# Spectral filter and gated MLP on one core: side work dealt out over more gaps, a block's low parts in one VectorE operation

## The chip, the core and the metric

One core of a Trainium2 chip runs the whole program. The metric is device time in microseconds (us) from a run of the compiled kernel, the median over several runs. Beside them stands one profiled execution, whose trace gives every duration below.

## The reference

The input `A_x` has 2048 tokens of 576 features. Two branches are mixed by a gate for each token:

```
g = sigmoid((x * gate_w).sum(-1, keepdims=True))
a = irfft2(rfft2(x) * (w_r + 1j * w_i), s=(2048, 576))
b = (gelu(x @ w_gate) * (x @ w_up)) @ w_down        # 576 -> 4608 -> 576, gelu by tanh
out = g * a + (1 - g) * b
```

## The kernel before, in words

**TensorE and its precision.** Every matmul of the MLP is done on operands split into a high part, rounded to the format of the fast matmul, and a low part, the rest. Three matmuls (high by high, low by high, high by low) stand for one. So every operand, weights, tokens and hidden values alike, must first be split: ScalarE copies the high part (`copy`, line 238), VectorE subtracts it from the source for the low part.

**Passes, tiles, blocks.** The tokens are worked in two passes of 1024 (p = 0, 1). The 36 tiles of 128 hidden features go in 18 pairs i. The first pairs of a pass (3 in the first, 7 in the second, `FIRST`) are *normal*: for each half tb of the tokens, `hidden` runs 14 matmuls for the gate and 14 for the up product of a tile, then GELU, product and split follow on ScalarE and VectorE. All later pairs are *blocks* (`products`): a Strassen-like scheme takes seven products of 2x2 block combinations in place of eight, named a11, a12, s2, s3, a22, s1, s4, in this order (n = 0 to 6, two halves s of seven matmuls each, `seven`, line 1178). The weights' combinations are made by `Block.prep` (line 1153): `total` adds quadrants on VectorE (line 1165), `high` copies 768 columns on ScalarE, `rest_of` makes the low parts on VectorE, 512 columns at line 1172 and a half-height piece of 256 columns at line 1173. There are three slots for such weights, and product m+2 is prepared while m runs. The tokens' combinations are made once for a pass by `operands` and `other_operands`, and the last one, s4, by `last_operand` just before the first block.

**Down projections.** `down` multiplies one 128-token part of the hidden values by two `dn` tiles: 12 matmuls of 288 columns into a `pdn` bank, ScalarE scales the result by 1-g into a `stg` tile (line 938), and GpSimd's queue adds it to the tile's sum `yd` in DRAM (line 920).

**The spectral branch** is side work, with no matmuls but for the column transform: `gate_part` and `other_gates` make the gates of the two halves, `forward_rows` the row transforms (VectorE), `send_away` puts rows into DRAM as `away`, `columns` takes them back as `til`, does the column transform with matmuls at line 300 and the filter, `inverse_rows` goes back and adds a to `yd`.

**The order is written out by hand** (a manual schedule): each engine runs its instructions in the order in which the program issues them. `gap()` (line 707) is called after every seven matmuls or so and counts time in gaps. `at(n, fn)` puts a step n gaps later, `seq` a chain of such steps, `due` runs what is left of a chain before its result is needed. The generator of the side work (`gens`) is advanced in a gap while `credit` is positive: TensorE's time times `RATE` 1.08 is put in, VectorE's costs are taken out, and what is saved up is capped at 3.0 us. `waits(n)` lets the generator pass n gaps. A second list, `side`, is served when the generator only waits. An instruction whose operand is late holds what is written behind it for its engine. SyncE's queue (SP) issues nearly all loads and stores in the same manner, and a `dma_start` whose buffer is not free yet holds the loads behind it.

**Kept low parts.** `lows` are DRAM tiles in which the first pass stores low parts of weights (`lower`, line 792): those of all 36 `dn` tiles, and of the first six `gub` tiles. The second pass loads them back on GpSimd's queue (line 796) instead of computing them.

## Time and profile before

| | |
|---|---|
| runs | 1398.64 us median of 3 (1397.9 to 1405.32) |
| profiled execution | 1401.8 us, its span 1400.0 us |
| busy share of the span | TensorE 96%, VectorE 83%, ScalarE 57%, GpSimd 21% |
| instructions | 20396, of them 7322 matmuls and 7322 weight loads |
| DMA | 272.12 MB, mean 194 GB/s; GpSimd's queue 44.7% and SP's 34.6% of the DMA engines' time |

How to read it: PE is TensorE, PEld its weight load, DVE VectorE, ACT ScalarE, POOL GpSimd, SP SyncE. In a group's row stand the line, the engine, the operation, the tiles written and read, shapes and count, then busy us and mean ns of one, then the engine's idle time just before them and what ended most of it. In a timeline row stand the start, the duration, engine, line, operation and count, and in brackets the idle time before it with what ended it. PEclk is the granted share of TensorE's clock. The spans of matmuls overlap, so TensorE counts as busy also where its clock is halved.

### The profile page before, as it was taken

The numbers are of one execution on the slowest core, as the hardware profiler recorded it, in microseconds if no ns is written. First come the engines' busy times: TensorE is split into PE (matmuls) and PEld (weight loads), VectorE is DVE, ScalarE is ACT, GpSimd is POOL, SyncE is SP. The second block draws the span as 40 slices with busy tenths as digits, with TensorE's granted clock in tenths as the row PEclk, the third lists the DMA queues.
The fourth block names the chain that finished last, engine by engine and source line by source line (L and its number), as shares of the span: only waits on it lengthen the run. The fifth ranks groups of instructions, "written<-read, shape, count | busy, mean of one in ns | idle before, by whom it ended". The sixth has DMA issues, their size and how long they took to land.

```text
span 1400.0 us, 20396 instructions
## 1 busy us (share of the span) xinstructions
PE 1349.6 (96%) x7322; PEld 1177.7 (84%) x7322; DVE 1166.2 (83%) x1772; ACT 797.4 (57%) x1302; POOL 287.3 (21%) x370
## 2 busy tenths in 40 slices
PE   9998999989999999999999999999899998999998
PEld 7887888878888888878888878888688887888887
DVE  6998999779999988766388767879889966999994
ACT  5557556545565566676556555743565575556552
POOL 0021111112111111111302222221122241222231
PEclk9999999999999999999999999999999999999999
DMA  9785667867777678988989999868667788667798
GB/s 338 246 170 101 137 143 175 237 194 147 147 147 147 147 181 225 282 219 225 309 276 279 234 235 238 208 140 248 196 144 141 144 166 215 118 145 147 147 211 227
DMA packets 119237, 272.12 MB, mean 194 GB/s; under 512 B 14560, under 2 KB 24800, under 8 KB 116832
## 3 DMA queue, kind: packets, MB, share of 16 engines
q0 software_dynamic: 48864, 106.06, 44.7%
q1 hardware_dynamic: 70272, 164.76, 34.6%
q8 instruction: 57, 0.93, 0.3%
q14 instruction: 44, 0.36, 0.1%
HBM read 144.43 MB, written 119.19 MB: 188 GB/s over the span
## 4 chain that ended last, share of the span: by engine, by line
PE 60%; DVE 16%; issue 11%; DMA 7%; ACT 4%; POOL 2%; SPq 0%; DVEq 0%; ACTq 0%; POOLq 0%
PE pdn L907 20%; PE pgu L1186 14%; PE px L1186 11%; PE pgu L1188 2%; DMA tmp<-xg 2%; PE px L1188 2%; PE pgu L828 2%; PE pgu L829 2%; PE pgu L830 2%; DVE gub L1172 2%; DMA ext<-til 1%; PE px L828 1%; PE px L829 1%; PE px L830 1%; DMA til<-ext 1%
## 5 line engine op out<-in xcount | busy, mean ns | idle before, releaser
L920 POOL DMA_DIRECT2D yd<-stg x264 | 226.4, 879 | 1045.6 <-ACT stg L938 1013.4
L938 ACT ACTIVATE stg<-pdn,omg 128x576 f32<-128x576 f32 x276 | 200.8, 737 | 213.5 <-PE pdn L907 196.1
L907 PEld LDWEIGHTS pdn<-dn,hb 128*128 128x128 f32 x2184 | 304.5, 188 | 11.4 <-DVE low L969 0.4
L907 PE MATMUL pdn<-dn,hb 128*128 128x288 f32 x2184 | 312.8, 294 | 0.1
L1186 PE MATMUL pgu<-xhi,gub 128*128 128x512 f32 x624 | 202.3, 405 | 26.2 <-ACT gub L238 11.1
L238 ACT ACTIVATE gub<-low 128x768 fp32r<-128x768 f32 (+3 forms) x180 | 155.7, 865 | 22.5 <-DVE low L1165 11.7
L1186 PE MATMUL px<-til,gub 128*128 128x512 f32 x624 | 160.7, 393 | 3.3 <-ACT xraw L238 3.3
L1186 PEld LDWEIGHTS pgu<-xhi,gub 128*128 128x128 f32 x624 | 114.5, 192 | 54.0 <-ACT gub L238 12.9
L1186 PEld LDWEIGHTS px<-til,gub 128*128 128x128 f32 x624 | 114.1, 188 | 27.5 <-ACT xraw L238 6.3
L1186 PE MATMUL pgu<-xlo,gub 128*128 128x512 f32 x312 | 124.6, 399 | 0.0
L1172 DVE TENSOR_TENSOR gub<-low,gub 128x512 fp32r<-128x512 f32 x156 | 107.3, 688 | 10.4 <-ACT gub L238 8.9
L907 PE MATMUL pdn<-dn,ext 128*128 128x288 f32 x624 | 100.8, 295 | 1.8 <-DVE ext L892 1.8
L907 PE MATMUL pdn<-dn,gub 128*128 128x288 f32 x624 | 99.9, 296 | 1.7 <-ACT stg L938 1.7
L907 PEld LDWEIGHTS pdn<-dn,gub 128*128 128x128 f32 x624 | 93.0, 189 | 7.7 <-ACT stg L938 1.9
L828 PE MATMUL pgu<-xhi,gub 128*128 128x512 f32 x240 | 93.9, 391 | 0.0
L829 PE MATMUL pgu<-xhi,gub 128*128 128x512 f32 x240 | 93.9, 391 | 0.0
L830 PE MATMUL pgu<-xlo,gub 128*128 128x512 f32 x240 | 93.6, 390 | 0.0
L907 PEld LDWEIGHTS pdn<-dn,ext 128*128 128x128 f32 x624 | 88.7, 188 | 2.9 <-DVE ext L892 2.9
L1186 PE MATMUL pgu<-til,gub 128*128 128x512 f32 x312 | 79.9, 391 | 0.0
L1218 DVE TENSOR_TENSOR xraw<-xraw,pgu 128x512 f32<-128x512 f32 x104 | 69.6, 682 | 8.4 <-PE pgu L1188 8.4
L1165 DVE TENSOR_TENSOR low<-low 128x768 f32<-128x768 f32 x75 | 71.5, 955 | 1.3
L1186 PEld LDWEIGHTS pgu<-xlo,gub 128*128 128x128 f32 x312 | 60.3, 193 | 13.8
(211 smaller groups left out, 2464.7 us busy)
## 6 DMA issues: line engine op xcount, KB each, us to landing
yd<-stg POOLq DMA_DIRECT2D x264, 288.0 KB, 5.3
low<-ws SPq DMA_DIRECT2D x87, 384.0 KB, 5.7
gub<-wd SPq DMA_DIRECT2D x52, 288.0 KB, 4.0
low<-wgu SPq DMA_DIRECT2D x17, 640.0 KB, 7.2
lo<-dn SPq DMA_DIRECT2D x36, 288.0 KB, 5.4
dn<-lo POOLq DMA_DIRECT2D x36, 288.0 KB, 6.6
rows<-col POOLq DMA_DIRECT2D x32, 256.0 KB, 7.2
gub<-ws SPq DMA_DIRECT2D x17, 384.0 KB, 6.2
```

Of the source, the lines that this page charges most:

```text
L238: act.activation(o, i, AF.Copy)
L828: pe.matmul(ps, w[:, 0, k, c], xhi[tb][:, k], start=k == 0, stop=False)
L829: pe.matmul(ps, w[:, 1, k, c], xhi[tb][:, k], start=False, stop=False)
L830: pe.matmul(ps, w[:, 0, k, c], xlo[tb][:, k], start=False, stop=False)
L907: pe.matmul(ps[half], h[:, l, c], d[:, q, half * HD:(half + 1) * HD], start=part == 0 and n == 0, stop=part == 1 and n == 2)
L920: pl.dma_start(yd[u], o, accum_op=ALU.add)
L938: put(u, lambda o: act.activation(o.rearrange("p (c k) -> p c k", c=2), v[:, :, 0:HD], AF.Copy, scale=omg[:, u:u + 1]), i == 0)
L1165: vec.tensor_tensor(o, p, q, ALU.subtract)
L1172: vec.tensor_tensor(w[:, 768:1280], x[:, 0:512], f(w[:, 0:512]), ALU.subtract)
L1186: pe.matmul(ps, l[:, c], x[:, t], start=first and t == 0 and q == 0, stop=False, skip_group_check=True)
L1188: pe.matmul(ps, w[:, 512 + P * s:512 + P * (s + 1)], xt, start=False, stop=True, skip_group_check=True)
L1218: vec.tensor_tensor(o, o, v, ALU.add)
```

## The change

- `Block.prep`: the low parts are laid out so that one VectorE operation of 3x256 columns writes all of them. For this the high part is copied by two ScalarE operations, 2x256 columns and 256 columns scaled by a column of the mask `msk` (0 for the upper half of the partitions, 1 for the lower).
- First block of a pass: products 0, 1 and 2 are prepared during the last normal pair (leads 0, 2 and 4) in place of 0 in that pair, 1 at its end and 2 within the block. `last_operand` takes seven gaps in place of three.
- `finish` in the blocks: product and split of the hidden values are put one or two gaps later, except for c22 and the last pair. The high copies of a block's `dn` tiles move from n = 2, 3 to n = 4, 5.
- Gates of the second half are made from the `rows` tile that was loaded for the row transform, with strided reads. The separate loads `xg` are gone. The gates of the first half run beside `operands` as side work, and the first operand loads `xs` are issued earlier, ahead of the weight loads of tiles 2 and 3.
- `split`, `tails_of` and `other_operands` issue one step of each kind in a gap, and the stores of `other_operands` and `send_away` are issued two gaps after the work that makes them. The cap on saved-up credit is 2.0 in place of 3.0.
- `away` is one DRAM tile. `til` comes back in four loads by digit, put 1, 6, 18 and 26 gaps after product 5 of the last block of the first pass; before, it came in four contiguous loads after that block. The column transform may start 14 gaps after that point. Weight loads for tiles NT+2 and NT+3 come later.
- `inverse_rows` of the second half waits 13 and 9 gaps for its two loads, in place of 6 and 6.
- `lows` keeps only `dn` tiles 14 to 35. In the second pass the low parts of `gub` tiles 0 to 5 and `dn` tiles 0 to 13 are computed.

The matmuls and their order are the same.

```diff
-        away = [dram.tile([P, 4 * SW], F32, name=f"away{i}", tag=f"away{i}") for i in range(6)]
+        away = dram.tile([P, 16 * SW], F32, name="away", tag="away")
+        spilt = [dram.tile([P, 4 * SW], F32, name=f"spilt{i}", tag=f"spilt{i}") for i in range(2)]
...
-                nc.sync.dma_start(away[2 * h + e], tmp[:, 0:4 * SW])
-                yield from waits(5)
+                at(2, lambda e=e: nc.sync.dma_start(away[:, 4 * SW * (2 * h + e):4 * SW * (2 * h + e + 1)],
+                                                    tmp[:, 0:4 * SW]))
+                yield from waits(7)
...
                 for e in range(2):
-                    nc.sync.dma_start(tmp[:, 0:4 * SW], away[4 + e])
-                    yield from waits(6)
+                    nc.sync.dma_start(tmp[:, 0:4 * SW], spilt[e])
+                    yield from waits(9 if e else 13)
...
-            gw = tmp[:, 0:D]
-            xg = [tmp[:, D * (1 + i):D * (2 + i)] for i in range(3)]
+            gw = tmp[:, D:2 * D]
             nc.sync.dma_start(gw, a["gw"][0:1, :].to_broadcast([P, D]))
-            for t in range(3):
-                nc.sync.dma_start(xg[t], a["xg"][t])
-            yield from waits(5)
+            yield from waits(9)
+            one, fin = gate_part(1, gw)
             for t in range(8):
-                gate_sum(8 + t, xg[t % 3], xg[t % 3], gw)
-                yield 0.78
-                if t + 3 < 8:
-                    at(1, lambda t=t: nc.sync.dma_start(xg[t % 3], a["xg"][t + 3]))
-                yield None
-            gate_part(1)[1]()
+                one(t)
+                yield 1.33
+            fin()
...
-            side.append(forward_rows())
-            yield from operands()
-            yield from side.pop()
             yield from send_away(0)
...
-            credit[0] = min(credit[0], 3.0)
+            credit[0] = min(credit[0], cap[0])
...
-        lows = [[dram.tile([P, n], F32, name=f"lo{j}_{n}", tag=f"lo{j}_{n}") if n == D or j < KEPT else None
-                 for n in (KT * 256, D)] for j in range(NT)]
+        lows = {j: dram.tile([P, D], F32, name=f"lo{j}", tag=f"lo{j}") for j in range(2 * FIRST[1], NT)}
...
         def split(xs, his, los):
-            for x, h in zip(xs, his):
-                copy(h, x)
-            yield None
-            yield None
-            for x, h, l in zip(xs, his, los):
-                vec.tensor_tensor(l, x, f(h), ALU.subtract)
-                yield 0.72
+            for k in range(len(xs) + 2):
+                if k < len(xs):
+                    copy(his[k], xs[k])
+                if k > 1:
+                    vec.tensor_tensor(los[k - 2], xs[k - 2], f(his[k - 2]), ALU.subtract)
+                    yield 0.72
+                yield None
...
             for i in range(3):
-                yield from sums(1, i, cells[0:5], [fr(c) for c in cells[8:11]])
-                xs, his = [cells[q] for q in (3, 0, 2)], [fr(c) for c in cells[5:8]]
-                nc.sync.dma_start(four_d[:, TB * i:TB * (i + 1)], cells[4])
+                q, h = quads[i], [fr(c) for c in his[i]]
...
                 if i == 2:
+                    out += [(kept[3 + n], cells[8 + n]) for n in range(3)]
+                    yield from tails_of(list(zip(h, xs)))
+                    out += [(kept[n][:, 2048:], f(h[n])) for n in range(3)]
+                else:
+                    yield from split(xs, h, [fr(x) for x in xs])
                     for n in range(3):
-                        nc.sync.dma_start(kept[3 + n], cells[8 + n])
-                    yield from tails_of(list(zip(his, xs)))
-                    for n in range(3):
-                        nc.sync.dma_start(kept[n][:, 2048:], f(his[n]))
-                else:
-                    los = [fr(x) for x in xs]
-                    yield from split(xs, his, los)
-                    for n in range(3):
-                        nc.sync.dma_start(kept[n][:, TB * i:TB * (i + 1)], f(his[n]))
-                        nc.sync.dma_start(kept[n][:, 1024 + TB * i:1024 + TB * (i + 1)], f(los[n]))
-                    yield from waits(3)
+                        out += [(kept[n][:, TB * i:TB * (i + 1)], f(h[n])),
+                                (kept[n][:, 1024 + TB * i:1024 + TB * (i + 1)], xs[n])]
+                at(2, lambda out=out: store(out))
+                if i == 0:
+                    at(6, lambda: load_xs(1, 2, quads[2]))
+            yield from waits(3)
...
-            def high():
-                for i in range(2):
-                    copy(hi[:, i], fourth[i])
-                next(todo), next(todo)
-
-            def rest_of():
-                for i in range(2):
-                    vec.tensor_tensor(lo[:, i], fourth[i], f(hi[:, i]), ALU.subtract)
-                    credit[0] -= 0.72
-                for _ in todo:
-                    pass
-
-            at(1, high)
-            at(3, rest_of)
+            def high(i):
+                copy(hi[:, i], fourth[i])
+
+            def low(i):
+                vec.tensor_tensor(lo[:, i], fourth[i], f(hi[:, i]), ALU.subtract)
+                credit[0] -= 0.72
+
+            def tail(n):
+                for _ in range(n):
+                    next(todo, None)
+
+            at(1, lambda: tail(2))
+            at(2, lambda: high(0))
+            at(3, lambda: high(1))
+            at(4, lambda: tail(2))
+            at(6, lambda: [tail(2), low(0)])
+            at(7, lambda: low(1))
...
                 def high():
-                    copy(w[:, 0:768], x)
+                    copy(w[:, 1:4:2], x[:, 0:3:2])
+                    act.activation(w[:, 2], x[:, 1], AF.Copy, scale=msk[:, 1:2])
 
                 def rest_of():
-                    vec.tensor_tensor(w[:, 768:1280], x[:, 0:512], f(w[:, 0:512]), ALU.subtract)
-                    vec.tensor_tensor(w[64:128, 512:768], x[64:128, 512:768], f(w[64:128, 512:768]), ALU.subtract)
-                    credit[0] -= 1.15
+                    vec.tensor_tensor(w[:, 0:5:2], x, f(w[:, 1:4]), ALU.subtract)
+                    credit[0] -= 1.0
 
...
-                    seq((name, p, i), (1, gelu), (2, mult), *split_h(o, hold, wants))
+                    soon = 0 if name == "c22" or end else 1
+                    high, low = (fn for _, fn in split_h(o, hold, wants))
+                    seq((name, p, i), (1, gelu), (2 + soon, mult), (4 + soon - end, high), (5 + 2 * soon, low))
...
-                b.prep(i + m // 7, m % 7)
+                if n or i > b.first:
+                    b.prep(i + m // 7, m % 7)
+                if n == 0 and i > b.first:
+                    b.load_d(i)
+                if p and n in (1, 2):
+                    lower(("dn", j + n - 1), dn[(j + n - 1) % 4], None, 0)
+                if n in (4, 5):
+                    w, x = dn[(j + n - 4) % 4], b.wdr[n - 4]
+                    copy(w[:, 0], x)
+                    if p == 0:
+                        lower(("dn", j + n - 4), w, x, 0.76)
+                if n == 3 and i == b.first:
+                    b.more()
                 if n == 0:
                     b.load(i + 1, "r11", "r21")
-                if n in (2, 3):
-                    w, x = dn[(j + n - 2) % 4], b.wdr[n - 2]
-                    copy(w[:, 0], x)
-                    lower(("dn", j + n - 2), w, x, 0.76)
-                if n == 3 and i == b.first:
-                    b.more()
-                if n == 4:
-                    due(("dn", j))
-                    due(("dn", j + 1))
-                    b.load_d(i + 1)
...
+            if n == 5:
+                til = mk("til", [16 * SW])
+                there, here = (x.rearrange("p (e d k) -> p d e k", d=4, e=4) for x in (away, til))
+                for d, n in enumerate((1, 6, 18, 26)):
+                    at(n, lambda d=d: nc.sync.dma_start(here[:, d], there[:, d]))
+                back[0] = count[0] + 14
             if n == 6:
                 load_w(NT + 1)
-                load_w(NT + 2)
...
-        for j in range(2):
-            at(11 + j, lambda j=j: nc.sync.dma_start(lows[j][0], f(gub[j][:, KT * 256:])))
-        aux += [lambda: None] * 2
+        aux += [lambda: None, lambda: load_xs(0, 0, [xraw[:, q] for q in range(4)])]
...
         for i in range(2):
             aux.append(lambda i=i: [prep_dn(i), due(("dn", i)), load_w(i + 2)])
-        aux += [lambda: None] * 4
-
-        def branch():
-            one, fin = gate_part(0)
+        def gates():
+            one, fin = gate_part(0, gwb)
             for t in range(8):
                 one(t)
                 yield 1.33
             fin()
             for u in range(4):
-                at(max(1, 26 + u - count[0]), lambda u=u: release(u))
+                at(max(1, 22 + u - count[0]), lambda u=u: release(u))
+            yield from forward_rows()
+
+        def branch():
+            at(4, lambda: side.append(gates()))
+            yield from operands()
+            yield from side.pop()
             yield from spectral()
 
         aux.append(lambda: gens.append(branch()))
...
             if last and tb == 1:
                 b.wide()
-                b.prep(b.first, 0)
+                for m in range(2):
+                    b.prep(b.first, m, 2 * m)
...
+            if last and tb == 1:
+                b.prep(b.first, 2, 4)
             h1, key1 = hidden(j + 1, tb, mid)
...
                 b.load_d(b.first)
-                b.prep(b.first, 1)
                 last_operand()
...
-                til = mk("til", [16 * SW])
-                for e in range(4):
-                    at(3 + 2 * e, lambda e=e: nc.sync.dma_start(til[:, 4 * SW * e:4 * SW * (e + 1)], away[e]))
                 for n in range(6):
                     down(*pend.pop(0))
                     if n == 2:
+                        load_w(NT + 2)
                         prep_dn(NT)
                         prep_gu(NT + 1)
                         prep_dn(NT + 1)
-                        load_w(NT + 3)
-                back[0] = count[0] + 12
+                        at(6, lambda: load_w(NT + 3))
```

On the ScalarE queue at the opening of the first pass's blocks (the names `gub_70` and `gub_71` are the weight slots of the block products, `xhi_64` and `xtl_68` the parts of s4, `px` a copy of a product that frees its bank), before:

```order
L238 ACTIVATE hb_81<-gl_83 128x512
L238 ACTIVATE xhi_64<-ext 128x512 x2
L238 ACTIVATE xtl_68<-xraw 128x512
L238 ACTIVATE px_1146<-pgu 128x512
L238 ACTIVATE gub_70<-low 128x768
L238 ACTIVATE gub_71<-low 128x768
L238 ACTIVATE px_1147<-pgu 128x512
```

and with the change:

```order
L931 ACTIVATE stg_86<-pdn,omg 128x576
L238 ACTIVATE gub_70<-low 128x2x256
L1188 ACTIVATE gub_70<-low,msk 128x256
L113 ACTIVATE tmp<-rows 128x320 x2
L238 ACTIVATE gub_71<-low 128x2x256
L1188 ACTIVATE gub_71<-low,msk 128x256
L931 ACTIVATE stg_87<-pdn,omg 128x576
L113 ACTIVATE tmp<-rows 128x320 x2
L124 ACTIVATE rows<-tmp 128x20x8
L125 ACTIVATE rows<-tmp 128x20x8
L931 ACTIVATE stg_88<-pdn,omg 128x576
L238 ACTIVATE hb_81<-gl_83 128x512
```

The copies of the weights for products 1 and 2 moved from behind the copies for s4 to ahead of two evacuations of down projections (`stg_87`, `stg_88`) that precede the block.

On VectorE, at the same place, before (line 1172 and line 1173 make the low parts of a block product, line 93 is a butterfly of the row transform, line 1165 a combination of quadrants):

```order
L93 TENSOR_TENSOR tmp<-rows 128x1280
L1165 TENSOR_TENSOR low<-low 128x768 x2
L93 TENSOR_TENSOR rows<-rows 128x40x32
L1172 TENSOR_TENSOR gub_70<-low,gub_70 128x512
L1173 TENSOR_TENSOR gub_70<-low,gub_70 64x256
L1165 TENSOR_TENSOR low<-low 128x768
```

and with the change, where the low parts of product 1 are the row of line 1191:

```order
L127 SCALAR_TENSOR_TENSOR rows<-rows,tmp 128x20x8
L885 TENSOR_TENSOR hb_80<-gl_82,hb_80 128x512
L1191 TENSOR_TENSOR gub_70<-low,gub_70 128x3x256
L129 SCALAR_TENSOR_TENSOR rows<-rows,tmp 128x20x8
L863 TENSOR_TENSOR gl_83<-gl_83,pgu 128x512
```

The low parts of product 1 moved from behind two butterflies to ahead of the last up product's multiplication (`gl_83`).

On SP's queue around the load of the second half's rows (`xn`), before:

```order
L571 DMA away_98<-tmp 128x2320
L653 DMA rows<-xn 128x4608
L660 DMA tmp<-gw 128x576
L662 DMA tmp<-xg 128x576 x3
L803 DMA lo_576_146<-dn_75 128x576
L1148 DMA gub_1143<-wd 128x576 x2
L1143 DMA low<-ws 128x768
L668 DMA tmp<-xg 128x576
```

and with the change:

```order
L571 DMA away<-tmp 128x2320
L654 DMA rows<-xn 128x4608
L660 DMA tmp<-gw 128x576
L1155 DMA low<-ws 128x768
L1155 DMA gub_1111<-ws 128x768
```

The eight loads `xg` are gone, and the block's quadrants (`ws`) follow the rows directly.

83 lines of the change are left out of this document (53 added, 30 removed).

## The prediction

> **What bounds the kernel now.** I read the page's head first, then who waited for whom on TensorE, then the granted clock, then the timeline at each long wait.
>
> ```profile
> span 1400.0 us, 20396 instructions
> PE 1349.6 (96%) x7322; PEld 1177.7 (84%) x7322; DVE 1166.2 (83%) x1772; ACT 797.4 (57%) x1302; POOL 287.3 (21%) x370
> ```
>
> TensorE is the bound, and the change leaves its 7322 matmuls as they are. So a gain can only come out of time in which TensorE stands still or runs at half clock. The waits of TensorE alone, longest in total first:
>
> ```profile
> PE pgu L1186 <- ACT gub L238: 11.1, 7, 3.1
> PE px L300 <- ACT til L238: 7.4, 10, 1.6
> PE px L1186 <- ACT xraw L238: 5.9, 7, 2.1
> PE pgu L1186 <- DVE gub L1172: 5.6, 2, 4.1
> PE pgu L1186 <- ACT px L238: 5.1, 1, 5.1
> PE pgu L1186 <- ACT ext L238: 2.9, 4, 1.0
> PE pdn L907 <- DVE ext L892: 1.8, 3, 0.9
> ```
>
> These seven rows make 39.8 us; the rows below them are 1.7 us and less each, some 5.6 us in all. The windows view, asked for the four stretches at half clock, gives the rest (columns: the stretch, its length, busy time of PE, PEld, DVE, ACT and POOL, granted clock, DMA share, GB/s):
>
> ```profile
> 123.33:130.16 6.83, 5.82 (x14) 4.57 (x15) 6.71 (x11) 2.27 (x4) 0.00 (x0) 0.50 0.07 12
> 297.41:300.82 3.41, 3.41 (x10) 2.65 (x9) 3.37 (x7) 0.28 (x1) 0.29 (x1) 0.50 0.94 287
> 986.90:993.73 6.83, 5.49 (x13) 4.33 (x14) 6.70 (x11) 1.62 (x3) 0.00 (x0) 0.50 0.63 238
> 1171.22:1178.05 6.83, 5.07 (x15) 4.39 (x16) 6.45 (x12) 3.84 (x7) 1.73 (x2) 0.50 0.57 169
> ```
>
> TensorE was busy 19.8 us in them at clock 0.50, so half of that, 9.9 us, is lost to the clock. Waits and clock together are 45.4 + 9.9 = 55.3 us, 4% of the span: this is what there is to win. Each half-clock stretch follows one long wait, and the timeline shows what was late there. Opening of the blocks, first pass:
>
> ```profile
> 119.34 1.14 ACT L238 ACTIVATE xhi<-ext 128x512 fp32r<-128x512 f32 x2
> 120.38 0.62 ACT L238 ACTIVATE xtl<-xraw 128x512 fp32r<-128x512 f32 x1
> 121.42 1.74 ACT L238 ACTIVATE gub<-low 128x768 fp32r<-128x768 f32 x2
> 122.30 0.51 PE L1186 MATMUL pgu<-xhi,gub 128*128 128x512 f32 x1 [3.13 <-ACT gub L238]
> 124.34 0.80 PE L1186 MATMUL pgu<-xhi,gub 128*128 128x512 f32 x1 [1.54 <-DVE gub L1172]
> ```
>
> The weights of product 1 are copied after three copies for s4, which is needed only at n = 6. TensorE waits 3.13 us for the copy and 1.54 us for the low part. Second pass, same place:
>
> ```profile
> 983.65 0.50 PE L1186 MATMUL pgu<-xhi,gub 128*128 128x512 f32 x1 [1.37 <-ACT gub L238]
> 988.24 0.79 PE L1186 MATMUL pgu<-xhi,gub 128*128 128x512 f32 x1 [4.09 <-DVE gub L1172]
> ```
>
> The third is the return of the second half's rows, the fourth the gates of the second half:
>
> ```profile
> 1163.78 0.33 SPq L621 DMA_DIRECT2D tmp<-away  x1
> 1170.68 1.77 ACT L238 ACTIVATE rows<-tmp 128x289 f32<-128x289 f32 x3 [5.99 <-DMA tmp<-away]
> 1172.98 1.22 PE L1186 MATMUL pgu<-xhi,gub 128*128 128x512 f32 x2 [5.08 <-ACT px L238]
> ```
>
> ```profile
> 291.98 0.76 DVE L736 SCALAR_TENSOR_TENSOR tmp<-tmp 128x576 f32<-128x576 f32 x1 [4.89 <-DMA tmp<-xg]
> 294.56 0.63 ACT L238 ACTIVATE gub<-gl 128x512 fp32r<-128x512 f32 x1 [4.94 <-DVE gl L1204]
> 295.95 0.70 PE L1186 MATMUL pgu<-xhi,gub 128*128 128x512 f32 x2 [2.80 <-ACT gub L238]
> ```
>
> In both, side work that waits for a load stands at the head of an engine's queue, and a copy that TensorE needs stands behind it.
>
> **The change part by part.** *A, B: openings.* Products 0 to 2 are now prepared within the last normal pair, and in the order shown with the change the copies for products 1 and 2 stand ahead of two evacuations of down projections, before any copy for s4. VectorE's low parts for product 1 stand ahead of the last up product. Both lie matmuls of several us ahead of their use. The waits that go: 3.13 + 1.54 = 4.67 us and 1.37 + 4.09 = 5.46 us. Late next would be the third product's combinations (line 1165), but these moved along.
>
> *C: return.* The first load was issued at 1163.78, and data came at 1170.68, 6.9 us later. The reader is put 7 gaps further on. A gap holds seven matmuls, about 1.6 us, so the reader moves by 11 us against a wait of 5.99 us. 5.08 us go.
>
> *D: gates.* The loads `xg` vanish, and eight reads of `rows` take their place, which cost more each:
>
> ```profile
> L736 DVE SCALAR_TENSOR_TENSOR tmp<-rows,low 128x576 f32<-128x576 f32 x8 | 10.4, 1304 | 0.2
> L736 DVE SCALAR_TENSOR_TENSOR tmp<-tmp 128x576 f32<-128x576 f32 x8 | 6.1, 756 | 8.0 <-DMA tmp<-xg 8.0
> ```
>
> That is 8 x 0.55 = 4.4 us more of VectorE, hidden since VectorE idles 8.0 us there now. The load of rows lands long before: nine gaps of waiting are 14 us, and that load took 12.4 us. 2.80 us of TensorE's wait go. With the clock, A to D hold 4.67 + 5.46 + 5.08 + 2.80 + 9.9 = 27.9 us. I take 25, leaving about 0.7 us of waiting at each place.
>
> [...]
>
> *E: the other waits.* In the seven rows there remain ScalarE's copies of weights 11.1 - 3.13 - 1.37 - 2.80 = 3.8 us, `xraw` 5.9, `ext` 2.9 (line 238) and 1.8 (line 892): 14.4 us. They come from steps of different kinds issued together (`finish`, `split`, `other_operands`, stores that hold SP's queue), which the change spreads, while the waits of `send_away` on GpSimd's memset stay. Bounds 0 and 14.4 us; I take half, 7 us.
>
> *F: block preparation.* The durations that the new operations are nearest to:
>
> ```profile
> L1172 DVE TENSOR_TENSOR gub<-low,gub 128x512 fp32r<-128x512 f32 x156 | 107.3, 688 | 10.4 <-ACT gub L238 8.9
> L1173 DVE TENSOR_TENSOR gub<-low,gub 64x256 fp32r<-64x256 f32 x156 | 65.9, 422 | 4.5
> L1165 DVE TENSOR_TENSOR low<-low 128x768 f32<-128x768 f32 x75 | 71.5, 955 | 1.3
> L238 ACT ACTIVATE gub<-low 128x768 fp32r<-128x768 f32 x156 | 130.6, 837 | 13.9 <-DVE low L1165 11.7 <-PE px L1188 2.1
> L238 ACT ACTIVATE hb<-gl 128x512 fp32r<-128x512 f32 x66 | 41.5, 628 | 28.6 <-DVE gl L1204 28.3 <-DVE gl L870 0.3
> L238 ACT ACTIVATE gub<-low 128x256 fp32r<-128x256 f32 x5 | 2.1, 414 | 3.7 <-DMA low<-wgu 3.6
> ```
>
> The groups of 156 have a second group of 26 from another tile, so 182 preparations. VectorE: one operation of 768 columns, 0.955 us by the nearest row, for 0.688 + 0.422 = 1.110 us: 182 x 0.155 = 28 us less. ScalarE: 0.628 + 0.414 = 1.04 us for 0.837, 182 x 0.205 = 37 us more (the mask's scale can add to it). ScalarE then has 834 of some 1367 us, 61%. Neither is on TensorE's path by itself: the copy is put two gaps, 3.2 us, ahead of the low part, which has another gap or more in hand. So 0, with what a tighter ScalarE could do among the rivals.
>
> *G: low parts.* Twenty loads on GpSimd's queue and twenty stores go, 14 of 288 KB and 6 of 640 KB each way, 16 MB of 272. In return the second pass computes them on VectorE:
>
> ```profile
> L800 DVE TENSOR_TENSOR gub<-low,gub 128x1280 fp32r<-128x1280 f32 x12 | 17.9, 1493 | 1.2 <-ACT gub L238 1.2
> L800 DVE TENSOR_TENSOR dn<-low,dn 128x576 fp32r<-128x576 f32 x6 | 4.5, 758 | 0.0
> 775.00:900.00 125.00, 117.58 (x664) 102.55 (x663) 89.85 (x146) 70.80 (x124) 30.31 (x43) 1.00 0.98 237
> ```
>
> 6 x 1.49 + 14 x 0.76 = 19.6 us over some 260 us, where VectorE is busy 89.85 of 125 us in the stretch shown: covered. In that stretch the DMA engines are busy 0.98, and the column transform's waits (7.4 us, line 300) come from short transfers among the long ones. Fewer bytes help; an earlier start beside the reload of `til` does not. Bounds -4 and +4 us; I take +1.
>
> *H: start.* Four loads `xs` of 256 KB now precede the weights of tiles 2 and 3, on which ScalarE waits already:
>
> ```profile
> 28.77 1.28 ACT L238 ACTIVATE gub<-low 128x1280 fp32r<-128x1280 f32 x1 [0.93 <-DMA low<-wgu]
> 37.77 0.65 ACT L238 ACTIVATE stg<-pdn 128x576 f32<-128x576 f32 x1 [4.13 <-PE pdn L907]
> ```
>
> At 338 GB/s, the page's rate for the first slice, 1.05 MB are 3.1 us. ScalarE idles 4.13 us before 37.77, so most is absorbed. Bounds 0 and 4 us of loss; I take 1.
>
> Sum: 25 + 7 + 1 - 1 = 32 us. The profiled execution took 1401.8 us, 3.2 us over the median of the runs; against the median, 1398.6 - 32 = **1366 us**, about 1368 us of span.
>
> **The rivals.** (1) *Stalls trade places.* Only the openings are clean, 10.1 us of waits and (5.82 + 5.49) / 2 = 5.7 us of clock; what is saved at C to E comes back a few gaps later, since VectorE is full (6.71 of 6.83 us busy in the first half-clock stretch). 1398.6 - 15.8 = 1383 us. For it: VectorE has 20 us more work in the second pass. Against: a block now asks it for less.
>
> (2) *ScalarE becomes the late one (slower).* Within a block, product s3 writes the bank that `xraw` is copied from, and those waits (5.9 us, seven times) show the copy queued behind others. Each copy of weights now takes 0.2 us more ahead of it. If each of the 26 blocks came to wait as those seven did, 0.84 us, at two products, that is 44 us, less the 32: 1411 us. It decides once the queue ahead of that copy is longer than the 1.6 us of a down projection that lies between. Against: ScalarE at 61%, and the weights' copies sit two gaps ahead.
>
> (3) *The seam of the passes gets worse (no change).* `til` returns earlier beside the token loads, and the weights of tiles NT+2 and NT+3 are loaded later, so that ScalarE waits for them as in the row at 28.77. Each such wait of 5 to 6 us with its half clock costs as much as C, 5.08 + 2.5 = 7.6 us; three of them undo 23 of the 32 us, and with E at nothing the time is 1397 us. Against: in that stretch before, TensorE hardly waited though DMA was full.
>
> (4) *All goes*: 27.9 + 14.4 + 4 + some of the short waits, 48 us, 1350 us.
>
> **How the numbers follow.** Forecast 0.58 (1356 to 1377 us), rival 1 0.20, rival 4 0.07, rival 3 0.08, rival 2 0.07. The range reaches from rival 4 nearly to the old time, 1348 to 1392 us, which leaves rivals 2 and 3 out. A measurement here can tell 0.5%, 7 us, from no change: faster than 1391.6 us 0.85, within 0.08, slower 0.07.
>
> **What would show it.** Right: no half-clock stretch near 120, 985 and 1165 us; line 1186's wait for `gub` under 3 us; VectorE's block operation near 0.96 us and some 28 us less busy time before the added low parts; no row `tmp<-xg`. Wrong: a new wait over 2 us of TensorE behind ScalarE's weight copies within blocks (rival 2), loads of `wgu` that end ScalarE's idle time near 660 to 700 us (rival 3), or line 300's waits grown well over 7.4 us.

## The result and the profile after

The changed kernel takes 1352.22 us, median of four runs (1349.49 to 1353.94), against 1401.05 us of the kernel before in the same runs (1397.9 to 1405.32). The ratio is 0.9648, with a 95% interval from 0.9612 to 0.9683. That is 48.8 us less. The prediction had said 32 us less and 1366 us; 1352 us lies in its range of 1348 to 1392 us, near the rival in which everything goes (1350 us), and below the 1356 to 1377 us that it had held likeliest.

The head of the page of the changed kernel:

```profile
span 1349.4 us, 20304 instructions
PE 1333.0 (99%) x7322; PEld 1173.3 (87%) x7322; DVE 1141.9 (85%) x1610; ACT 836.3 (62%) x1484; POOL 275.7 (20%) x350
```

TensorE, which was at 96%, is at 99% of a span that is 50.6 us shorter. Its waits, longest in total first, with four rows of 0.3 to 0.6 us left out before the last (line 1203 was 1186, line 900 was 907):

```profile
PE px L1203 <- DVE gub L1191: 3.2, 2, 2.0
PE pdn L900 <- ACT stg L931: 1.9, 2, 1.8
PE px L1203 <- ACT xraw L238: 1.8, 2, 1.0
PE pgu L1365 <- DVE gate L1361: 1.5, 1, 1.5
PE pgu L1203 <- DVE xraw L1237: 1.0, 1, 1.0
...
PE px L300 <- ACT til L238: 0.2, 1, 0.2
```

Some 45 us of waits have become 11. The groups, with the new block preparation first and one of ScalarE's copies of hidden values last:

```profile
L1191 DVE TENSOR_TENSOR gub<-low,gub 128x768 fp32r<-128x768 f32 x156 | 148.5, 952 | 17.0 <-ACT gub L1188 15.8 <-PE px L1205 1.2
L238 ACT ACTIVATE gub<-low 128x512 fp32r<-128x512 f32 x156 | 97.7, 626 | 19.5 <-DVE low L1181 19.0
L1188 ACT ACTIVATE gub<-low,msk 128x256 fp32r<-128x256 f32 x156 | 77.8, 499 | 0.0
L238 ACT ACTIVATE ext<-xraw 128x512 fp32r<-128x512 f32 x26 | 16.2, 622 | 0.0
```

The durations came out as estimated: 0.952 us for 0.955 on VectorE, 0.626 and 0.499 us on ScalarE, which overlap by 0.1 us so that the pair takes 1.02 us, for 1.04. ScalarE's busy time rose by 38.9 us (37 were expected).

TensorE's matmuls can be matched one by one between the two traces, since there are as many of them and the order is the same but for those of the column transform (the description of the change says that nothing moved, which is right for all the others). The transform's products come in rounds of about 52 tile matmuls. In the changed kernel they come one such round earlier, and for most of the transform one gap later within the round. The difference of the two starts of a tile's matmul, read at the edges of a stretch (so for the transform at its two ends), says what the stretch gave back:

| term of the prediction | stretch of before | taken | gave back |
|---|---|---|---|
| A opening, pass 1 | 110 to 140 us | | 6.6 |
| B opening, pass 2 | 980 to 1010 | | 4.7 |
| C return of rows | 1160 to 1180 | | 7.7 |
| D gates | 290 to 340 | | 6.5 |
| A to D with the clock | | 25 | 25.4 |
| E other waits | 200 to 270, 370 to 615, 1040 to 1080, 1190 to 1250 | 7 | 18.2 |
| G columns | 690 to 920 | 1 | 6.8 |
| H start | 0 to 60 | -1 | -0.7 |

That is all but 0.3 us of the 50 us between the last matmuls. So A to D in sum and H were right in size, and the 17 us that were missing are E (11 us) and G (6 us). Which edit gave them back is another question; the table only says where. (The expectations below have 16.8 us for E; read at these edges it is 18.2.) The runs below ask it. Each puts some part of the change back into the changed kernel, so its time stands beside 1352.2 us.

### The profile page after: what moved, and what is told of

It is laid out like the page before. It is cut to its first block, busy times and chain, and to the rows that moved or that the text cites. A ratio compares the mean times of both kernels' runs of the same rounds, so it can differ in the third digit from the quotient of the medians.

```text
span 1349.4 us, 20304 instructions
## 1 busy us (share of the span) xinstructions
PE 1333.0 (99%) x7322; PEld 1173.3 (87%) x7322; DVE 1141.9 (85%) x1610; ACT 836.3 (62%) x1484; POOL 275.7 (20%) x350
## 4 chain that ended last, share of the span: by engine, by line
PE 84%; DVE 6%; ACT 3%; issue 2%; DMA 1%; DVEq 0%; ACTq 0%
PE pdn L900 29%; PE pgu L1203 20%; PE px L1203 15%; PE pgu L1205 3%; PE pgu L821 3%; PE pgu L822 3%; PE pgu L823 3%; PE px L1205 2%; PE px L300 1%; PE px L821 1%; PE px L822 1%; PE px L823 1%; DMA low<-wd 1%; PE pgu L827 1%; PE pgu L828 1%
## 5 line engine op out<-in xcount | busy, mean ns | idle before, releaser
L931 ACT ACTIVATE stg<-pdn,omg 128x576 f32<-128x576 f32 x276 | 204.6, 742 | 325.5 <-PE pdn L900 274.4
L1203 PE MATMUL pgu<-xhi,gub 128*128 128x512 f32 x624 | 194.2, 393 | 1.0 <-DVE xraw L1237 1.0
L1191 DVE TENSOR_TENSOR gub<-low,gub 128x768 fp32r<-128x768 f32 x156 | 148.5, 952 | 17.0 <-ACT gub L1188 15.8
L238 ACT ACTIVATE gub<-low 128x512 fp32r<-128x512 f32 (+3 forms) x180 | 122.8, 682 | 35.1 <-DVE low L1181 19.0
L1203 PE MATMUL pgu<-xlo,gub 128*128 128x512 f32 x312 | 121.5, 389 | 0.0
L1237 DVE TENSOR_TENSOR xraw<-xraw,pgu 128x512 f32<-128x512 f32 x104 | 70.7, 682 | 29.2 <-PE pgu L1205 28.9
L822 PE MATMUL pgu<-xhi,gub 128*128 128x512 f32 x240 | 93.9, 391 | 0.0
L821 PE MATMUL pgu<-xhi,gub 128*128 128x512 f32 x240 | 93.9, 391 | 0.0
L823 PE MATMUL pgu<-xlo,gub 128*128 128x512 f32 x240 | 93.4, 389 | 0.0
L1188 ACT ACTIVATE gub<-low,msk 128x256 fp32r<-128x256 f32 x156 | 77.8, 499 | 0.0
L238 ACT ACTIVATE xraw<-px 128x512 f32<-128x512 f32 x104 | 62.1, 597 | 22.1 <-PE px L1205 19.3
```

Source lines behind the costliest of these rows:

```text
L238: act.activation(o, i, AF.Copy)
L821: pe.matmul(ps, w[:, 0, k, c], xhi[tb][:, k], start=k == 0, stop=False)
L822: pe.matmul(ps, w[:, 1, k, c], xhi[tb][:, k], start=False, stop=False)
L823: pe.matmul(ps, w[:, 0, k, c], xlo[tb][:, k], start=False, stop=False)
L931: put(u, lambda o: act.activation(o.rearrange("p (c k) -> p c k", c=2), v[:, :, 0:HD], AF.Copy, scale=omg[:, u:u + 1]), i == 0)
L1188: act.activation(w[:, 2], x[:, 1], AF.Copy, scale=msk[:, 1:2])
```

## The experiments

### The openings put back

```diff
-                for m in range(2):
-                    b.prep(b.first, m, 2 * m)
+                b.prep(b.first, 0)
...
-            if last and tb == 1:
-                b.prep(b.first, 2, 4)
...
+                b.prep(b.first, 1)
                 last_operand()
...
-                if n or i > b.first:
-                    b.prep(i + m // 7, m % 7)
+                b.prep(i + m // 7, m % 7)
```

and the old `last_operand`, so that ScalarE's copies stand again in the order of the kernel before.

> The changed kernel with both openings put back: product 0 prepared in the last normal pair, 1 at its end, 2 within the block, and the three steps of the last operand in three gaps. Theory (terms A and B, each stall with its half clock): matched matmul by matmul, the two stretches around 120 and 985 us of the kernel before gave back 6.6 and 4.7 us, so the time is 1352 + 11 = 1363 us (1360 to 1368), with waits of line 1203 for gub of over 1 us and two half-clock stretches at the openings. Rival (the stalls there were made by a VectorE that the old block preparation kept full, and the order alone costs little): under 1357 us, and no half clock.

Measured: 1356.49 us (1355.28 to 1358.22), ratio to before 0.9688 (0.9671 to 0.9705). It costs 4.3 us, not 11. The timeline of TensorE at the two openings of this kernel:

```profile
121.31 0.50 PE L1200 MATMUL pgu<-xhi,gub 128*128 128x512 f32 x1 [0.73 <-ACT gub L238]
123.46 0.80 PE L1200 MATMUL pgu<-xhi,gub 128*128 128x512 f32 x1 [1.65 <-DVE gub L1188]
...
955.07 0.50 PE L1200 MATMUL pgu<-xhi,gub 128*128 128x512 f32 x1 [0.73 <-ACT gub L238]
958.43 0.50 PE L1200 MATMUL pgu<-xhi,gub 128*128 128x512 f32 x1 [2.87 <-DVE gub L1188]
```

With the very order that made waits of 3.13 + 1.54 and 1.37 + 4.09 us, the waits are now 0.73 + 1.65 and 0.73 + 2.87 us, and each is followed by 3.41 us at half clock in place of 6.83. So neither side is wholly right: the waits over 1 us and the two half-clock stretches are the theory's, the time, under 1357 us, is the rival's. More than half of what the openings gave back did not need their new order. Something else in the change had shortened these stalls; the next section has a part of the answer for the first opening.

### The blocks: preparation, spacing, cap

Three edits act in every block: the one VectorE operation of the preparation, the later product and split of hidden values (`finish`), and the cap of 2.0 us, which acts on side work everywhere. They were put back alone and together (the reads of the weights, and their order in memory, go back with the preparation; that is left out here):

```diff
+                    copy(w[:, 0:768], x)
...
+                    vec.tensor_tensor(w[:, 768:1280], x[:, 0:512], f(w[:, 0:512]), ALU.subtract)
+                    vec.tensor_tensor(w[64:128, 512:768], x[64:128, 512:768], f(w[64:128, 512:768]), ALU.subtract)
                     credit[0] -= 1.0
```
```diff
-                    soon = 0 if name == "c22" or end else 1
-                    high, low = (fn for _, fn in split_h(o, hold, wants))
-                    seq((name, p, i), (1, gelu), (2 + soon, mult), (4 + soon - end, high), (5 + 2 * soon, low))
+                    seq((name, p, i), (1, gelu), (2, mult), *split_h(o, hold, wants))
```
```diff
-        cap = [2.0]
+        cap = [3.0]
```

The preparation alone:

> The changed kernel with the old block preparation: one ScalarE copy of 768 columns, two VectorE operations for the low parts, the old layout of the weights. The books of the side work keep 1.0 us for it, so that every other step stays where it is. VectorE gets 28 us more to do, ScalarE 37 us less. Theory (the preparation costs nothing on TensorE's path, as the prediction took it; the waits of term E went through the spreading of steps): 1352 to 1356 us. Rival (the waits of E went because VectorE had room again): waits of TensorE for VectorE's tiles and for xraw come back, 1360 to 1369 us.

The spacing alone:

> The changed kernel with the product and split of a block's hidden values one to two gaps earlier, as before. Theory (waits for ext, xraw and weight copies within blocks came from these steps standing at the head of ScalarE's and VectorE's queues at once): some 6 of the 16.8 us that term E gave back are lost again, 1358 us (1356 to 1363), in single waits of 0.5 to 1.2 us for ext, xraw and gub. Rival (those waits came from side work issued together, and the spacing within blocks does nothing): 1351 to 1354 us.

Then the three together, since the first had cost more and the second less than the theory said:

> The changed kernel with three things put back at once: the old block preparation (two VectorE operations, books still at 1.0 us), the earlier product and split of hidden values, and the cap of 3.0 us on saved-up credit. Alone, the first cost 8 us and the second 0 to 3. Theory (each of them breaks up the same bunch of VectorE operations ahead of the product of the hidden values, so that any one covers for the others): more than the sum of the single costs, near the 16.8 us that term E gave back, 1369 us (1365 to 1373), with ScalarE's copies ext, gub and hb of hidden values waiting for VectorE and TensorE waiting behind them. Rival (VectorE's longer preparation is the whole of it): 1359 to 1363 us, as with the first alone.

And the pairs, to see who covers for whom:

> The changed kernel with the earlier product and split of hidden values and the cap of 3.0 us, but the new block preparation. The three together cost 32.5 us, the preparation alone 8, the spacing alone 3. Theory (VectorE's shorter preparation covers for the two others, since 1.0 in place of 1.1 us for each of seven products leaves it room to catch up): 1355 to 1362 us. Rival (the bunches are made by cap and spacing, the length of the preparation adds only its own 8 us): 1372 to 1378 us.

> The changed kernel with the old preparation and the earlier product and split, but the cap of 2.0 us. Theory (the cap of 2.0 keeps the bunches short, so the two cost what they cost alone, 8 + 3 us): 1361 to 1366 us; then the step from here to 1385 us is the cap's. Rival (preparation and spacing make the stalls between them whatever the cap): 1376 to 1386 us.

Measured (the two columns in the middle are ScalarE's idle time ahead of its 144 copies of a block's hidden values, `hb`, `gub` and `ext`, and how many of these waits are over 2.5 us):

| put back | ScalarE waits, us | over 2.5 us | time, us | cost, us | ratio to before |
|---|---|---|---|---|---|
| nothing (changed kernel) | 0.9 | 0 | 1352.2 | | 0.9648 (0.9612 to 0.9683) |
| spacing | 114.0 | 12 | 1355.6 | 3.4 | 0.9688 (0.9666 to 0.9710) |
| preparation | 2.7 | 0 | 1360.5 | 8.3 | 0.9712 (0.9695 to 0.9730) |
| spacing, cap | 129.2 | 18 | 1364.1 | 11.9 | 0.9740 (0.9718 to 0.9763) |
| preparation, spacing | 188.6 | 37 | 1370.6 | 18.4 | 0.9783 (0.9756 to 0.9811) |
| all three | 194.2 | 38 | 1384.8 | 32.5 | 0.9892 (0.9873 to 0.9911) |
| kernel before | 187.1 | 31 | 1401.0 | 48.8 | 1 |

The three together are worth 32.5 us, two thirds of the whole gain, and no theory on record had them that large. None is additive: the preparation costs 8.3 us alone, 18.4 - 3.4 = 15.0 with the spacing gone too, and 32.5 - 11.9 = 20.7 with spacing and cap gone. The cap costs 8.5 us beside the spacing and 14.2 us beside both. The spacing alone costs nothing that this many runs can tell: the intervals overlap, and its profiled span, 1349.5 us, is that of the changed kernel (which has a half-clock stretch of 3.41 us that this one lacks; the last section shows both). The preparation alone came out as its rival had it: TensorE's waits for VectorE's tiles grow from 5.2 to 8.7 us. In both of the pairs the time lies between theory and rival: each edit covers for the others, but only in part. The cap was not put back alone.

What it is that they cover for can be seen in the groups. ScalarE's copy `ext<-xraw` in the kernel before, then with the spacing alone put back, then with all three:

```profile
L238 ACT ACTIVATE ext<-xraw 128x512 fp32r<-128x512 f32 x26 | 16.4, 631 | 47.0 <-DVE xraw L1204 47.0
```
```profile
L238 ACT ACTIVATE ext<-xraw 128x512 fp32r<-128x512 f32 x26 | 16.4, 631 | 32.1 <-DVE xraw L1221 32.0
```
```profile
L238 ACT ACTIVATE ext<-xraw 128x512 fp32r<-128x512 f32 x26 | 16.4, 630 | 58.1 <-DVE xraw L1220 58.1
```

The high copy of the hidden values stands at the head of ScalarE's queue and waits for VectorE's product. With the new spacing it never does (0.0 in the changed kernel). The timeline with all three put back shows one such place:

```profile
507.61 0.80 DVE L92 TENSOR_TENSOR gub<-tmp 128x580 f32<-128x580 f32 x1
508.45 2.36 DVE L92 TENSOR_TENSOR tmp<-tmp 128x580 f32<-128x580 f32 x3
510.73 0.68 DVE L1188 TENSOR_TENSOR gub<-low,gub 128x512 fp32r<-128x512 f32 x1
511.44 0.42 DVE L1189 TENSOR_TENSOR gub<-low,gub 64x256 fp32r<-64x256 f32 x1
511.89 0.69 DVE L1220 TENSOR_TENSOR gl<-gl,px 128x512 f32<-128x512 f32 x1
512.62 0.63 ACT L238 ACTIVATE gub<-gl 128x512 fp32r<-128x512 f32 x1 [3.52 <-DVE gl L1220]
513.33 1.00 PE L1202 MATMUL pgu<-xhi,gub 128*128 128x512 f32 x2 [1.88 <-ACT gub L238]
```

Four butterflies of side work in a row (3.2 us, what a cap of 3.0 lets through at once), two operations of block preparation, and only then the product of the hidden values at 511.89. ScalarE waits 3.52 us for it, and TensorE starts 0.08 us after ScalarE's copy has ended, 1.88 us late. A stretch of 3.41 us at half clock follows. In the changed kernel the matmul of the same number starts with no wait. On VectorE, these stand ahead of it:

```profile
490.80 0.75 DVE L100 TENSOR_TENSOR tmp<-gub,tmp 128x580 f32<-128x580 f32 x1
491.47 0.95 DVE L1191 TENSOR_TENSOR gub<-low,gub 128x768 fp32r<-128x768 f32 x1
492.34 0.75 DVE L100 TENSOR_TENSOR tmp<-gub,tmp 128x580 f32<-128x580 f32 x1
493.01 0.68 DVE L1237 TENSOR_TENSOR xraw<-xraw,pgu 128x512 f32<-128x512 f32 x1
```

Single side operations lie between the steps of the block. TensorE's waits with all three put back:

```profile
PE pgu L1202 <- ACT ext L238: 6.4, 11, 1.4
PE pgu L1202 <- ACT gub L238: 5.3, 5, 2.1
PE px L1202 <- ACT xraw L238: 4.3, 6, 1.4
PE px L1202 <- DVE gub L1188: 4.0, 2, 2.3
PE pgu L1202 <- DVE xraw L1234: 3.0, 3, 1.4
```

These are the rows of term E over again, and larger. The reason why the edits back each other up is, by these traces, the slack: with the spacing alone put back, ScalarE waits 114 us at these copies and TensorE loses next to nothing; only 2 of the 144 waits are over 3.3 us, against 17 with all three put back. A wait cost TensorE time here only where it was longer than the work that TensorE had in hand. Each further edit moves more of the waits beyond it. The count over 2.5 us does not explain all: preparation with spacing (37) and all three (38) differ by 14.2 us. There TensorE's waits for `ext` are 2.5 and 6.4 us, those for `gub` 0.8 and 5.3 us, and the half-clock stretches ahead of the kernel's last microseconds two and four. Nor does the list of waits hold every stall: at full clock the row of a matmul of 512 columns lasts 0.39 us and the next starts 0.23 us later (0.227 in the median of the changed kernel and of the kernel before), so a short stall hides under the row. Starts 0.24 us and more apart at full clock, with no idle time between, stood 5.2 us in all beyond 0.22 us each in the kernel before (56 of them) and 0.8 us in the changed kernel (10).

Part of what the cap does can be placed. The kernels with the spacing put back, and with spacing and cap, differ in the cap alone. Matched with the changed kernel, the first loses nothing from 110 to 140 us and from 280 to 290 us, the second 3.7 and 3.6 us, each with a half-clock stretch. These are the first opening and the place of the gates, and the new order and the new gates are in both kernels. At the gates it is the chain of the kernel before, with no load `xg` in it:

```profile
286.65 0.63 ACT L238 ACTIVATE gub<-gl 128x512 fp32r<-128x512 f32 x1 [2.52 <-DVE gl L1221]
287.37 0.70 PE L1203 MATMUL pgu<-xhi,gub 128*128 128x512 f32 x2 [1.80 <-ACT gub L238]
```

So stalls at two of the places that the prediction laid to the order of the opening and to late loads come back with the larger cap.

### The return of the rows

```diff
-                    yield from waits(9 if e else 13)
+                    yield from waits(6)
```

> The changed kernel with waits of 6 and 6 gaps for the two loads of the second half's rows, in place of 13 and 9. Theory (term C: the reader of a load that is 6.9 us on its way stands at the head of ScalarE's queue, and the wait brings a half-clock stretch): a wait of TensorE near 5 us at about 1125 us and a half-clock stretch behind it, 1352 + 7.7 = 1360 us (1357 to 1362). Rival (with fewer bytes under way the load lands in time, or ScalarE's queue there holds nothing that TensorE needs): 1350 to 1355 us.

Measured: 1356.37 us (1354.87 to 1358.03), ratio 0.9691 (0.9673 to 0.9709), 4.1 us, between theory and rival. But hardly where the theory put it:

```profile
1106.23 0.33 SPq L622 DMA_DIRECT2D tmp<-spilt  x1
1111.92 1.31 DVE L543 TENSOR_TENSOR rows<-tmp 128x289 f32<-128x289 f32 x2 [6.74 <-DMA tmp<-spilt]
1116.30 0.70 PE L1203 MATMUL pgu<-xhi,gub 128*128 128x512 f32 x2 [0.91 <-ACT stg L931]
1299.55 0.70 PE L1203 MATMUL pgu<-xhi,gub 128*128 128x512 f32 x2 [2.65 <-DVE xraw L1237]
```

The load is still read too early: it lands 5.7 us after its issue, and VectorE waits 6.74 us for it, nearly as long as the 7.39 us before. TensorE loses 0.91 us, where it lost 5.08 us. The reader now falls on another product of the block, ScalarE has an evacuation to do in the meantime, and no half clock follows. Matched with the changed kernel, this place costs 1.2 us; another 3.7 us come up near 1300 us, where the side work ends eleven gaps earlier than in the changed kernel and VectorE is late once; elsewhere this kernel gains 1.3 us.

### The columns and the gates

```diff
-        lows = {j: ... for j in range(2 * FIRST[1], NT)}
+        lows = {("dn", j): ... for j in range(NT)}      # and ("gu", j) for j < 6
```

> The changed kernel with the low parts of gub tiles 0 to 5 and dn tiles 0 to 13 stored in the first pass and loaded in the second, as before: 16 MB more, some 20 us less of VectorE in the second pass. Theory (fewer long transfers beside the corner exchanges of the column transform are what took ScalarE's wait for til<-ext from 40 to 2.5 us): that wait is back over 20 us, line 300 waits 5 to 7 us, and the time is 1357 to 1360 us. Rival (the later weight loads and the earlier return of til did it): that wait stays under 10 us, and the time is 1350 to 1354 us.

Measured: 1354.48 us (1351.68 to 1361.13), ratio 0.9680 (0.9649 to 0.9710): not to be told from the changed kernel. ScalarE's wait for the corner exchanges, in the stretch of the column transform, is 3.7 us, so the bytes alone are not it (for most of its length this kernel's transform stands where it stands in the changed kernel). The next question was the place within the round: in the changed kernel it is, for most of the way, one gap later, since early in the transform there is no credit in one gap and the generator slips by that gap. The smaller cap is not the whole reason: with the cap of 3.0 put back (with the spacing, or with all three) the slip comes after 42 products in place of 6, and the rest stands one gap later all the same. Two kernels fix the place by serving the generator in every gap, the second after one more `waits(1)`:

```diff
+            if pace[0]:
+                credit[0] = max(credit[0], 0.01)
...
+            pace[0] = True
             for kb in range(16):
```

> The changed kernel with the column transform kept at one step in each gap whatever the credit. So it stands, product for product, at the same places among the matmuls of the tiles as in the kernel before; bytes, loads and low parts are those of the changed kernel. Theory (the place in the tile's rhythm decides whether the corner exchanges meet the long loads): ScalarE's wait for til<-ext is back above 15 us, line 300 waits 4 to 7 us, 1357 us (1355 to 1360). Rival (some other part of the change took the waits): that wait stays under 8 us, 1350 to 1354 us.

> As the run before, but one gap later: the column transform stands at the places among the tiles' matmuls at which it stands in the changed kernel for most of its length. Theory: ScalarE's wait for til<-ext under 8 us, line 300 waits under 2 us, 1351 to 1354 us, some 5 us less than one gap earlier. Rival: both runs alike within 2 us.

Measured: 1350.48 us (1348.52 to 1352.21), ratio 0.9645 (0.9628 to 0.9661), at the old place, and 1352.71 us (1350.83 to 1354.71), ratio 0.9661 (0.9644 to 0.9679), one gap later. Half of the theory stands: ScalarE's wait depends on the place. In the stretch from 690 to 870 us at the old place, and then one gap later:

```profile
ACT rows L238 <- DMA til<-ext: 28.8, 10, 6.7
```
```profile
ACT rows L238 <- DMA til<-ext: 2.1, 1, 2.1
```

The other half falls: line 300 waits 1.7 us in the first of them, and the time is no worse. So old place (one round earlier than in the kernel before, as in the changed kernel) and old bytes were put together, and in the same kernel, at another time, the old loads of the gates:

> The changed kernel with the column transform at the places of the kernel before (as in the run one gap earlier), the kept low parts stored and loaded as before, and the gates of the second half from eight separate loads as before. The parts lie apart in time: gates near 285 us, columns from 690 to 900 us. Theory for the columns (place and bytes together made the waits): ScalarE's wait for til<-ext near 40 us and 5 to 7 us of waits at line 300, where the place alone gave 29 and 1.7 us. Rival (the copies of weights and hidden values beside them did it): under 2.5 us at line 300. Theory for the gates (a load that is late at the head of VectorE's queue stops TensorE, term D): 5 to 7 us lost between 275 and 300 us. Rival (as at the openings, most of it went by the looser blocks): under 3 us. Time 1362 to 1366 us if both theories hold, 1352 to 1356 us if neither does.

Measured: 1365.18 us (1364.86 to 1366.58), ratio 0.9750 (0.9727 to 0.9773), 13.0 us. ScalarE's row in that stretch, and TensorE's two rows of line 300:

```profile
ACT rows L238 <- DMA til<-ext: 38.6, 10, 6.9
```
```profile
PE px L300 <- ACT til L238: 6.8, 5, 2.4
PE px L300 <- ACT rows L238: 2.1, 1, 2.1
```

At 8.9 us these are a little more than the 7.4 us of the kernel before. Neither the bytes (line 300 at 1.8 us) nor the place (1.7 us) makes them; both together do, by the same slack as in the blocks: at the old place all but one of ScalarE's waits are between 1.2 and 3.9 us, which TensorE does not feel, and with the additional loads every second one is 4.5 to 6.9 us. The stretch from 640 to 900 us costs 12.7 us in all, more than the 6.8 us that it had given back: to the waits at line 300 come two half-clock stretches, which the kernel before has not there, and 1.7 us of waiting for a kept low part of `gub`. As for the gates, the row of TensorE there is a wait of 1.94 us on VectorE, and the stretch from 280 to 320 us costs 2.3 us against the changed kernel, where it had given back 6.5 (no half clock follows the wait here). That is the rival's, under 3 us, and a stall that the larger cap makes at the same place is shown above; the two were not put back together. The time fits the range for both theories although one of them fell, which is luck: the columns cost more than their theory had.

### An attempt at less

At the second opening the changed kernel still waits 2.0 us and runs 3.41 us at half clock. What is late, by the order of the matmuls, are the low parts of the fourth product, s3 (the expectation calls it the third). One edit takes credit from the side work there:

```diff
                 b.wide()
+                credit[0] -= 3.0
```

> The changed kernel with 3.0 us taken from the credit of the side work at the point where the first block's products are prepared, in both passes, so that fewer of its operations stand ahead of the third product's low parts. Theory (the waits of 1.2 and 2.0 us of line 1203 for line 1191 at the openings, with the short half-clock stretch behind the second, go): 4 us less, 1348 us. Rival (the side work comes back a few gaps later and stalls there, or the wait is ScalarE's): 1351 to 1354 us.

Measured: 1351.11 us, median of four runs (1349.55 to 1352.64), ratio 0.9647 (0.9624 to 0.9671): the same time. The second opening gives 3.9 us, but at the first a new wait comes up,

```profile
121.05 1.08 PE L1203 MATMUL pgu<-xhi,gub 128*128 128x512 f32 x2 [1.87 <-ACT px L238]
```

with its half clock, and the seam of the passes, near 650 us, has another 2.1 us. Neither this kernel nor the one with the columns at the old place, 1350.48 us, beats the changed kernel beyond the intervals.

## Why the prediction was right in direction and short in size

- **What bounds the kernel**: right in kind: TensorE's standing still and its half clock were what there was to win. As a bound the 55 us were too low. The span fell by 50.6 us, the listed waits by 34 and the loss to the clock by 8; the other 8 us stand in no listed wait (4.4 of them are the starts counted above, 5.2 us against 0.8).
- **A to D**: 25 us taken, 25.4 us found at the four places. The sum came out in part by luck: B gave back 4.7 us where waits and half clock had held 8.2, D 6.5 where they had held 4.5. In B the step that failed is the look at what would be late next: the third product's weights did move along, but the fourth's low parts come late, with a wait of 2.01 us and 3.41 us at half clock. In the causes, what failed is that each stall was taken as the work of the one edit at that place. Put back one at a time, the openings cost 4.3 us, the return 1.2 us at its place, the gates 2.3 us, while the larger cap, with the new opening and the new gates, makes 3.7 us at the first opening and 3.6 us at the gates. For the second opening and the return no run shows what took the remaining part.
- **E**: 7 us taken as half of 14.4, 18.2 us found. The bound itself was too low, as short waits below the seven rows, and stalls that no row lists, went as well. The step that failed is the choice of half, on the ground that the steps "of different kinds issued together" are only spread by the change. The block edits together removed ScalarE's waits for VectorE's products, 187.1 us to 0.9.
- **F**: 0 us taken, 8.3 us measured alone and up to 20.7 us beside the other two edits. The step that failed is "Neither is on TensorE's path by itself". VectorE's operation of 0.158 us less (0.688 + 0.422 - 0.952 us) lies seven times in each block between a product of hidden values and what waits for it. Busy shares hide this: VectorE stood at 83% before and stands at 85% now.
- **G**: +1 us taken within -4 to +4, 6.8 us found. The mechanism was half right: short exchanges that are late among long transfers, as ScalarE's row of 44 to 2.5 us shows, but that the products would stand a gap later in the tiles' round was not seen. By the runs either this or the fewer bytes is enough to spare TensorE the waits at line 300. The DMA engines are as full as before, a share of 0.98 in both kernels. The windows view of the changed kernel, in the same part of the transform:

```profile
742.00:860.00 118.00, 117.27 (x657) 102.89 (x656) 93.44 (x154) 70.97 (x122) 27.93 (x39) 1.00 0.98 241
```

- **H**: -1 us taken, -0.7 found.
- **Rivals**: ScalarE late in blocks fell (836 us busy, and its waits on VectorE's products went from 187 to 1 us: its queue has more work and less standing). Stalls trade places fell in the large but is what the last attempt ran into. The seam of the passes lost nothing. *All goes*, at 1350 us, is near in time, and with 0.07 it had too small a chance; not all went (11 us of waits and one half-clock stretch are left), but E and G gave more than their bounds. What was missed is that preparation, spacing and cap work on many of the listed waits at once, so that these go or stay together.
- **The signs**: the block operation near 0.96 us, 28.9 us less of VectorE's block operations and the missing row `tmp<-xg` came as forecast, and none of the signs of being wrong did. But the half-clock stretch near 985 us is only halved, to 3.41 us, and the block matmuls' waits for `gub` are 3.2 us, now for VectorE, where under 3 had been said.

## What to carry to other kernels

In this kernel a stall was made by the length of a bunch ahead of one short step (at 507.61 us above, 3.2 us of butterflies and two operations of block preparation ahead of a product of 0.69 us, for which ScalarE waited 3.52 us), and the cap on side work, the gap more before a dependent copy, and the shorter operation all worked on the same bunch: their gains covered for each other when one was taken away and were far larger together (32.5 us) than one by one (8.3, 3.4). Here, then, such edits are to be priced as a group. When testing a change, do not conclude from undoing one part that the part does nothing. And ask of a wait not how long it is but how much work the bound engine has in hand: 114 us of ScalarE's waiting cost too little here to be told from noise, while the kernels with 37 and 38 waits over 2.5 us lost 18 and 32 us.

## What the runs showed of the hardware

The half clock came after shorter standstills than the longest ones of the kernel before (5.08 and 4.09 us) suggested, after 2.01 us in the changed kernel, and not each time. TensorE's second opening in the changed kernel, the wait and then the window behind it:

```profile
961.73 1.52 PE L1203 MATMUL px<-til,gub 128*128 128x512 f32 x3 [2.01 <-DVE gub L1191]
```
```profile
961.90:965.31 3.41, 3.41 (x9) 2.64 (x10) 3.38 (x5) 1.00 (x3) 0.89 (x1) 0.50 0.44 46
```

and the same wait at the same time of the kernel with only the spacing put back:

```profile
961.69 1.43 PE L1203 MATMUL px<-til,gub 128*128 128x512 f32 x5 [1.98 <-DVE gub L1191]
```
```profile
961.90:965.31 3.41, 3.41 (x18) 2.88 (x18) 3.41 (x5) 2.70 (x6) 0.89 (x1) 1.00 0.46 49
```

A standstill of 2.01 us brought 3.41 us at clock 0.50 in the one and 1.98 us none in the other, half as many matmuls against twice as many (9 and 18). In the traces of the kernel before and of the changed kernel such a difference goes with the place of the standstill in a fixed rhythm. In both, all changes of the clock up to the last matmul lie whole multiples of 3.413 us behind the first record of the clock: at 34, 36, 85, 86, 287, 289, 341 and 343 of them in the kernel before, at 280 and 281 (955.73 us and 3.41 us more) in the changed kernel. Cut at these marks, the stretch ahead of the half clock in the changed kernel, and the two over which a wait of 2.06 us at 616 us is spread in the kernel before, where no half clock follows:

```profile
958.48:961.90 3.42, 1.41 (x10) 1.07 (x9) 3.42 (x6) 3.38 (x7) 0.00 (x0) 1.00 0.61 245
```
```profile
616.22 0.73 PE L1186 MATMUL px<-xhi,gub 128*128 128x512 f32 x2 [2.06 <-ACT xraw L238]
```
```profile
611.44:614.85 3.41, 2.71 (x17) 2.26 (x15) 1.39 (x3) 3.33 (x6) 0.85 (x1) 1.00 0.60 78
614.85:618.26 3.41, 2.04 (x9) 1.72 (x10) 1.87 (x3) 3.39 (x7) 0.00 (x0) 1.00 1.01 331
618.26:621.68 3.42, 3.42 (x22) 3.09 (x21) 1.11 (x2) 0.88 (x2) 0.85 (x1) 1.00 1.00 287
```

TensorE stands idle 2.01 us within one stretch here, but 0.70 and 1.37 us in two stretches there. The two traces hold 790 such stretches at full clock that end before the last matmul does. The five with the most idle time, 1.95, 2.01, 2.91, 2.91 and 3.32 us, were each followed by half clock, and none of the others was, of which the next had 1.62 us. How the 1.98 us of the kernel with only the spacing put back lie to its marks was not shown. The half clock lasted one such stretch or two (3.41 or 6.83 us). In the three places of the kernel before where it was two, TensorE was idle 1.01, 1.34 and 1.76 us in the first of them. Where it was one, it was idle 0.00 us at the gates of the kernel before and at the second opening of the changed kernel, and 0.16 and 0.00 us behind the two openings put back.

An estimate for pricing, from these rows: a wait of 2 us cost 1.7 us more (half of 3.41) where it fell into one stretch, which is luck, and so did two short ones close together (0.73 + 1.65 us at the first opening put back, 2.2 us of which lie in the 3.41 us ahead of its half clock).
